# Second batch's keys and values in the places of eight weight tiles, and a softmax constant added by ScalarE

## The chip, the cores and the metric

One core of one Trainium2 chip runs the whole program. The metric is device time in microseconds (us) of one execution, as the median of several runs. A profile is one further execution, recorded instruction by instruction; its span runs from the first to the last instruction.

## The reference

```python
# B, H, S, D = 8, 8, 576, 64; pool = 8; Sp = 72
k_p = k.reshape(B, H, Sp, pool, D).mean(axis=3)
v_p = v.reshape(B, H, Sp, pool, D).mean(axis=3)
scores = scale * np.matmul(q, k_p.transpose(0, 1, 3, 2))
attn = np.exp(scores - np.max(scores, axis=-1, keepdims=True))
attn = attn / (np.sum(attn, axis=-1, keepdims=True) + 1e-09)
x = np.matmul(attn, v_p)              # -> (4608 tokens, 512)
h = np.maximum(np.maximum(x @ w1, x @ w2), x @ w3)    # 768 wide
x = h @ w_out                                         # 512 wide
h = np.maximum(x @ w_in, 0.0)                         # 2048 wide
out = h * h @ w_out2
```

The expert weights arrive as 64-bit numbers, which the kernel converts itself.

## The kernel before

**Three stages in one stream.** The 4608 tokens are cut into 12 blocks of 384. For block j, `attention(j)` (line 293) makes four x tiles, one per pair of heads; `moe1(j)` (line 529) multiplies them by w1, w2 and w3 (18 weight tiles, `w1_f_e` in the pool `w_p`, 6 chunks f by 3 matrices e), takes the maximum, and multiplies by the output weights `wo1` (6 tiles). Later stages (line 612 on) run the second expert layer with 512-token blocks and start when the first stage is done; the change doesn't touch them. A matmul product is split in three: high by high, high by low and low by high (`PARTS`), since every operand is held as a high half, rounded by ScalarE (line 135), and a low half, which is the rest (line 136, by VectorE, for weights by GpSimd).

**Weights.** A weight tile is loaded raw (line 147, 512 KB, 64-bit integers) on SP's queue, into one of four places `raw0` to `raw3`. `convert` (line 150) turns it into floats with two ScalarE operations (lines 162 and 163) and two VectorE operations (lines 164 and 167), and `split` makes the two halves. While `shared[0]` is true, that is until the last output weight has been loaded, the four raw places go round in turn for weights, keys and values together (`place`, line 127).

**Attention.** A block holds pieces of one batch or two: block 0 is the first 384 tokens of batch 0, block 1 the last 192 of batch 0 and the first 192 of batch 1, block 2 the rest of batch 1. Batch 0's values are pooled by matmuls (line 264). From batch 1 on, `load_k` (229) and `load_v` (234) load one pair's keys (288 KB) and values (288 KB), `prepare_k` (239) sums groups of eight on VectorE (line 241) and scales them into `kbd` on ScalarE (244), and `prepare_v` (246) does the like for values (lines 248, 215 and 216). `softmax` (359) computes scores on TensorE (367), the maximum on VectorE (369), and exponentials with their sums on ScalarE (372, one activation and one read of its accumulator per tile and head). Then come the added constant (376) and the reciprocal (377) on VectorE, and the product of both on GpSimd (378). `transpose` (lines 399 and 408) and `values` (426 for batch 0, 437 and 438 later) make the x tile. The 64 softmaxes have 64 of the added constants. Ahead of the second layer's weights, the program also converts those and stores them (from line 451 on), in the course of blocks 2 to 11.

**What sets the order.** All steps go into the list `todo` with a due time in matmul steps of a block (`STEPS` is 22, of which 18 are weight tiles and four output columns) and are emitted in that order; loads lead their softmax by `LEAD_LOAD` = 10 steps. The framework's scheduler then orders the instructions of each engine from its own model of their costs, so a changed cost or a changed dependence moves instructions far from the edit. Each engine, SP's queue too, runs its own list strictly in order. A tile of a pool with a tag takes the place of the tile that had the tag before, and its writer waits until that one's readers are done.

Of the kernel before, what the change touches and what calls it, by code (L numbers as in the profile page):

```python
# [10 lines left out]
F32 = mybir.dt.float32  # L11
# [3 lines left out]
AF = mybir.ActivationFunctionType  # L15
# [5 lines left out]
P = 128  # L21
B, H, S, D = 8, 8, 576, 64
POOL = 8
SP = S // POOL
NPAIR = H // 2
# [4 lines left out]
KF1 = FF1 // P  # L30
FF2 = 2048
KF2 = FF2 // P
NE = 3
# [52 lines left out]
def as_f32(ap):  # L86
    return ap.bitcast(F32)
# [8 lines left out]
def attention_moe_kernel(ctx: ExitStack, tc: tile.TileContext, q, k, v, vn, w1, w2, w3, wo1, wi2, wo2, out):  # L96
    nc = tc.nc
# [29 lines left out]
    def place(kind):  # L127
        if shared[0]:
            turns["both"] += 1
            return f"raw{turns['both'] % 4}"  # L130
        turns[kind] += 1
        return f"raw{2 * kind + turns[kind] % 2}"
# [48 lines left out]
    w_p = s1.enter_context(tc.tile_pool(name="w_p", bufs=1))  # L181
# [6 lines left out]
    raw_p = s_at.enter_context(tc.tile_pool(name="raw_p", bufs=4, side="right"))  # L188
# [35 lines left out]
    def early(shape, name):  # L224
        if unused:
            return w_p.tile(shape, F32, tag=unused.pop(0), name=name)
        return raw_p.tile(shape, F32, tag=place(1), name=name, bufs=1)

    def load_k(b, p):
        kr = raw_p.tile([P, 2 * 512], F32, tag=place(1), name="kr", bufs=1)[:, :S]  # L230
        nc.sync.dma_start(out=kr, in_=k[b, p])
        return kr

    def load_v(b, p):
        vr = raw_p.tile([P, 2, D, POOL], F32, tag=place(1), name="vr", bufs=1)[:SP]
        nc.sync.dma_start(out=vr, in_=v[b - NATURAL, :, 2 * p : 2 * p + 2])
        return vr

# [7 lines left out]
    def prepare_v(p, vr):  # L246
        vs = sm_p.tile([SP, 2, D], F32, tag="vs", name="vs", bufs=2)
        nc.vector.tensor_reduce(out=vs, in_=vr, axis=AX.X, op=ALU.add)
        split_scaled(vst[:, p, 0:4:3], vst[:, p, 1:3], vs, V_SCALE)
# [75 lines left out]
    def scores(g):  # L325

        if not used or used[-1][1] + g > 3:
            used.append([sm_p.tile([P, 3, 2, SP], F32, tag="ss", name="ss", bufs=3), 0])
        used[-1][1] += g
        return used[-1][0][:, used[-1][1] - g : used[-1][1]]  # L330

    def attend(j, b, s0, n, p, t):

        kr, vr, qr, pt, sms = [], [], [], [], []
# [3 lines left out]
        def load():  # L338
            if j == 0:
                kq = early([P, 2 * 512], "kq")  # L340
                kr.append(kq[:, :S])
                qr.append(kq[:, S : S + n])
                nc.sync.dma_start(out=kr[0], in_=k[b, p])
            elif first:
                kr.append(load_k(b, p))
            if j:
                qr.append(raw_p.tile([P, T1], F32, tag="qr", name="qr", bufs=4)[:, :n])
            nc.sync.dma_start(out=qr[0], in_=q[b, p, :, s0 : s0 + n])
            if first and b >= NATURAL:
                vr.append(load_v(b, p))  # L350
# [8 lines left out]
        def softmax():  # L359
            if vr:  # L360
                prepare_v(p, vr.pop())
            g = len(tiles)
            sc = sc_ps.tile([P, 3 * 2 * SP], F32, tag="sc", name="sc")
            ss = scores(g)[:m]
            src = sc[:, : g * 2 * SP].rearrange("p (g h s) -> p g h s", h=2, s=SP)[:m]
            for i, (c, _) in enumerate(tiles):
                nc.tensor.matmul(src[:, i], lhsT=qr[0][:, c : c + m], rhs=kbd[:, p], start=True, stop=True)  # L367
            st = sm_p.tile([P, 3, 3, 2], F32, tag="st", name="st")[:m, :, :g]
            nc.vector.tensor_reduce(out=st[:, 0], in_=src, axis=AX.X, op=ALU.max, negate=True)  # L369
            for i in range(g):  # L370
                for h in range(2):
                    nc.scalar.activation(  # L372
                        ss[:, i, h], src[:, i, h], AF.Exp, bias=st[:, 0, i, h : h + 1],
                        accum_out=st[:, 1, i, h : h + 1],
                    )
            nc.vector.tensor_scalar_add(st[:, 1], st[:, 1], 1e-9)
            nc.vector.reciprocal(st[:, 2], st[:, 1])  # L377
            nc.gpsimd.tensor_tensor(  # L378
                out=ss, in0=ss,
                in1=st[:, 2].rearrange("p g (h o) -> p g h o", o=1).to_broadcast([m, g, 2, SP]), op=ALU.mult,  # L380
            )
            sms.append(ss)
# [36 lines left out]
        def values():  # L419
# [22 lines left out]
            split(x, xf)  # L442

        return load, prepare, softmax, carry, transpose, values

    w1_t, wo1_t = {}, {}
# [454 lines left out]
```

## Time and profile before

| | us |
|---|---|
| median of 3 runs (1459.45 to 1472.45) | 1459.91 |
| the profiled execution | 1462.14 |
| its span, first to last instruction | 1459.7 |
| TensorE matmuls busy in the span | 1425.5 |
| VectorE | 977.9 |
| ScalarE | 759.4 |
| GpSimd | 182.9 |

In the profile PE is the matmul side of TensorE and PEld its weight loads, DVE is VectorE, ACT is ScalarE, POOL is GpSimd and SPq the queue of DMA issues on SyncE. A matmul in plain fp32 counts as two instructions in the trace. Matmuls overlap, so the busy time of one is longer than its share; the count of instructions per microsecond tells more. PEclk is the TensorE clock that was granted, as a share of 2.4 GHz. The weights of the first layer are converted in the first 115 us, while blocks 0 and 1 are computed.

### The profile page before, as it was taken

To read this page: it belongs to the slowest core of one execution; us is meant where nothing else is said; L and a number is where in the kernel's file an instruction comes from. 1 tells how busy PE (TensorE), PEld (TensorE's weight loads), DVE (VectorE), ACT (ScalarE), POOL (GpSimd) and SP (SyncE) were. 2 spreads that over 40 slices of the span, in tenths; PEclk is the share of its full clock that TensorE was granted. 3 is DMA by queue.
4 is the path that set the end of the run, shared out by engine and by line. 5 is a ranking of instruction groups with operands and counts; after the bars stand their busy time and mean duration, and the time that the engine had idled before them with its cause. 6 is when DMAs were issued, how large, how long until landed. Compare 5 with 4: busy or idle time off the path is not lost.

```text
span 1459.7 us, 27670 instructions
## 1 busy us (share of the span) xinstructions
PE 1425.5 (98%) x10410; PEld 1403.0 (96%) x10410; DVE 977.9 (67%) x1754; ACT 759.4 (52%) x1959; POOL 182.9 (13%) x229
## 2 busy tenths in 40 slices
PE   6889999999999999999999999999999999999998
PEld 4879999999999999999999999999999999999998
DVE  5887477656675756646336767686867767686865
ACT  7795366655665657655223544453535444454543
POOL 3441022212322222221000000000000000000000
PEclk9989999999999999999999999999999999999999
DMA  7554145444455444433459747566566666555746
GB/s 226 182 169 141 62 143 180 162 140 142 146 180 177 149 148 142 133 120 107 167 190 355 290 160 256 186 223 222 209 221 224 232 231 221 204 217 199 258 153 209
DMA packets 125029, 272.81 MB, mean 187 GB/s; under 512 B 13504, under 2 KB 69568, under 8 KB 124896
## 3 DMA queue, kind: packets, MB, share of 16 engines
q1 hardware_dynamic: 117984, 261.61, 52.8%
q10 hardware_dynamic: 6912, 9.44, 1.8%
q8 instruction: 82, 1.34, 0.4%
q14 instruction: 51, 0.42, 0.1%
HBM read 213.91 MB, written 48.23 MB: 180 GB/s over the span
## 4 chain that ended last, share of the span: by engine, by line
PE 77%; DMA 5%; DVE 2%; ACT 1%; issue 1%; SPq 0%; POOL 0%; ACTq 0%; DVEq 0%; POOLq 0%
PE ps L701 23%; PE ps L541 22%; PE ps L560 8%; PE accB L825 6%; PE accA L825 6%; PE accE L825 3%; PE accF L825 3%; DMA wo2s<-wo_dram 3%; PE accD L825 2%; PE sc L367 2%; PE av L438 1%; PE av L437 1%; DMA wraw<-in_wi_dram 0%; PE tr L408 0%; DMA yr<-y_dram 0%
## 5 line engine op out<-in xcount | busy, mean ns | idle before, releaser
L541 PE MATMUL ps<-x,w 128*128 128x384 f32 x2592 | 491.0, 342 | 5.5 <-ACT w L135 3.0
L541 PEld LDWEIGHTS ps<-x,w 128*128 128x128 f32 x2592 | 452.0, 190 | 8.3 <-ACT w L135 3.4
L701 PE MATMUL ps<-y,wi2s 128*128 128x256 f32 x3024 | 372.8, 278 | 0.7 <-DVE a L672 0.2
L701 PEld LDWEIGHTS ps<-y,wi2s 128*128 128x128 f32 x3024 | 357.2, 188 | 2.4 <-DVE c L672 1.3
L560 PE MATMUL ps<-h,wo 128*128 128x384 f32 x864 | 159.0, 337 | 0.1
L560 PEld LDWEIGHTS ps<-h,wo 128*128 128x128 f32 x864 | 149.6, 188 | 0.3 <-ACT wo L135 0.2
L714 ACT ACTIVATE c<-c 128x512 f32<-128x512 f32 x90 | 56.3, 626 | 168.6 <-DVE c L672 168.0
L672 DVE TENSOR_TENSOR c<-ps,c 128x512 f32<-128x512 f32 x144 | 98.2, 687 | 66.4 <-PE ps L701 63.5
L549 DVE TENSOR_TENSOR hm<-ps,hm 128x384 f32<-128x384 f32 x144 | 79.7, 553 | 81.3 <-PE ps L541 78.8
L135 ACT ACTIVATE g<-c 128x512 fp32r<-128x512 f32 x144 | 90.3, 627 | 57.0 <-DVE c L711 23.3
L825 PE MATMUL accA<-wo2s,g 128*128 128x256 f32 x864 | 115.6, 277 | 0.0
L825 PE MATMUL accB<-wo2s,g 128*128 128x256 f32 x864 | 111.7, 279 | 3.9 <-DMA wo2s<-wo_dram 3.0
L372 ACT ACTIVATE ss<-sc,st 128x72 f32<-128x72 f32 (+1 forms) x320 | 97.8, 320 | 29.9 <-DVE st L369 24.8
L825 PEld LDWEIGHTS accB<-wo2s,g 128*128 128x128 f32 x864 | 104.5, 189 | 4.9 <-ACT g L135 2.2
L136 DVE TENSOR_TENSOR g<-c,g 128x512 fp32r<-128x512 f32 x144 | 97.8, 686 | 16.4 <-ACT g L135 16.4
L825 PEld LDWEIGHTS accA<-wo2s,g 128*128 128x128 f32 x864 | 107.0, 188 | 0.0
L441 DVE TENSOR_TENSOR xf<-av,xf 64x192 f32<-64x192 f32 (+1 forms) x112 | 50.7, 452 | 39.3 <-ACT xf L440 37.6
L378 POOL TENSOR_TENSOR ss<-ss,st 128x432 f32<-128x432 f32 (+1 forms) x64 | 53.1, 830 | 178.3 <-DVE st L377 95.0
L135 ACT ACTIVATE h<-hm 128x384 fp32r<-128x384 f32 x72 | 37.6, 522 | 56.2 <-DVE hm L549 55.5
L372 ACT ACTIVATION_READ_ACCUMULATOR ss<-sc,st 128x1 f32 (+1 forms) x320 | 66.2, 207 | 0.0
L135 ACT ACTIVATE g<-s 128x512 fp32r<-128x512 f32 x72 | 44.3, 630 | 35.3 <-DVE s L675 17.5
L163 ACT ACTIVATE wraw<-wraw 128x512 int32<-128x512 uint32 x56 | 37.8, 675 | 43.4 <-DMA wraw<-in_wi_dram 16.4
(111 smaller groups left out, 1929.2 us busy)
## 6 DMA issues: line engine op xcount, KB each, us to landing
wo2s<-wo_dram SPq DMA_DIRECT2D x252, 512.0 KB, 5.8
wi2s<-wi_dram SPq DMA_DIRECT2D x24, 512.0 KB, 6.5
wraw<-in_wo_dram SPq DMA_DIRECT2D x22, 512.0 KB, 3.9
wraw<-in_w_dram SPq DMA_DIRECT2D x18, 512.0 KB, 5.2
y_dram<-ys ACTq DMA_DIRECT2D x48, 192.0 KB, 2.7
wraw<-in_wi_dram SPq DMA_DIRECT2D x16, 512.0 KB, 3.7
wi_dram<-wraw SPq DMA_DIRECT2D x16, 512.0 KB, 3.0
wo_dram<-wraw SPq DMA_DIRECT2D x64, 128.0 KB, 2.1
```

The lines of the kernel that those rows point to most:

```text
L135: nc.scalar.activation(hi, src, AF.Copy)
L136: engine.tensor_tensor(out=lo, in0=src, in1=as_f32(hi), op=ALU.subtract)
L372: nc.scalar.activation(ss[:, i, h], src[:, i, h], AF.Exp, bias=st[:, 0, i, h : h + 1], accum_out=st[:, 1, i, h : h + 1],)
L378: nc.gpsimd.tensor_tensor(out=ss, in0=ss, in1=st[:, 2].rearrange("p g (h o) -> p g h o", o=1).to_broadcast([m, g, 2, SP]), op=ALU.mult,)
L441: nc.vector.tensor_tensor(out=xf[r], in0=av[r], in1=xf[r], op=ALU.add)
L541: nc.tensor.matmul(ps, lhsT=w1_t[f, e][:, a, kk * P : (kk + 1) * P], rhs=x[kk][:, c], start=(n == 0), stop=(n == 3 * KD - 1),)
L549: nc.vector.tensor_tensor(out=hm, in0=ps, in1=hm, op=ALU.max)
L560: nc.tensor.matmul(ps, lhsT=wo1_t[kk][:, a, d * P : (d + 1) * P], rhs=hs[kk][:, c], start=(n == 0), stop=(n == 3 * KF1 - 1),)
L672: nc.vector.tensor_tensor(out=out, in0=in0, in1=in1, op=ALU.add)
L701: nc.tensor.matmul(bank[:, u * HT : (u + 1) * HT], lhsT=wi2_t[2 * gr + u][i][:, a, o + kk * P : o + (kk + 1) * P], rhs=y_t[j][m][:, c, kk] ...
L714: nc.scalar.activation(c, c, AF.Relu)
L825: nc.tensor.matmul(bank[:, i * 256 : (i + 1) * 256], lhsT=g[:, a, u * HT + i * P : u * HT + (i + 1) * P], rhs=w[:, u, c], start=(n == 0 an ...
```

## The change

There are two edits. Batch 1's keys and values (4 pairs, 8 tiles) no longer take raw places: pair p's keys take the place of weight tile number 10 + 2p of the 18 and its values that of number 11 + 2p, which are `w1_3_1` to `w1_5_2`, before these weights are written. So that such a load isn't issued at the very start, `behind_weights` has GpSimd copy one element of the low half of weight tile number 2p (keys) or 2p + 1 (values) into the place first; the load waits for that copy. Later batches use the raw places as before. The second edit is in `softmax`: the constant 1e-9 is added by a ScalarE activation (Copy with a bias) instead of a VectorE addition.

```diff
+    def kv_place(b, i):
+
+        if b > 1:
+            return raw_p, place(1)
+        f, e = divmod(NE * KF1 - 2 * NPAIR + i, NE)
+        return w_p, f"w1_{f}_{e}"
+
+    def behind_weights(b, i, dst):
+        if b == 1:
+            nc.gpsimd.tensor_copy(dst, as_f32(w1_t[divmod(i, NE)][:1, 1, :1]))
+
     def load_k(b, p):
-        kr = raw_p.tile([P, 2 * 512], F32, tag=place(1), name="kr", bufs=1)[:, :S]
+        pool, tag = kv_place(b, 2 * p)
+        kr = pool.tile([P, 2 * 512], F32, tag=tag, name="kr", bufs=1)[:, :S]
+        behind_weights(b, 2 * p, kr[:1, :1])
         nc.sync.dma_start(out=kr, in_=k[b, p])
         return kr
 
     def load_v(b, p):
-        vr = raw_p.tile([P, 2, D, POOL], F32, tag=place(1), name="vr", bufs=1)[:SP]
+        pool, tag = kv_place(b, 2 * p + 1)
+        vr = pool.tile([P, 2, D, POOL], F32, tag=tag, name="vr", bufs=1)[:SP]
+        behind_weights(b, 2 * p + 1, vr[:1, 0, 0, :1])
         nc.sync.dma_start(out=vr, in_=v[b - NATURAL, :, 2 * p : 2 * p + 2])
         return vr
...
-            nc.vector.tensor_scalar_add(st[:, 1], st[:, 1], 1e-9)
+            nc.scalar.activation(st[:, 1], st[:, 1], AF.Copy, bias=1e-9)
             nc.vector.reciprocal(st[:, 2], st[:, 1])
```

From `load_k` on the lines of the changed kernel stand 10 to 15 higher than those of before; lines that the text names are those of before. The engines' orders change in many places up to the end of the first stage, and three of them follow. A name like `w_2_0_477` is weight tile f = 2, e = 0 with its buffer's number; `kr` is a load of keys, `vr` of values, `wraw` of raw weights, `qr` of queries.

SP's queue, from the first raw weights on, before:

```order
L147 DMA wraw<-in_w_dram 128x1024 x2
L348 DMA qr<-in_q_dram 128x192
L147 DMA wraw<-in_w_dram 128x1024 x2
L231 DMA kr<-in_k_dram 128x576
L348 DMA qr<-in_q_dram 128x192
L231 DMA kr<-in_k_dram 128x576
L236 DMA vr<-in_v_dram 72x1024
L147 DMA wraw<-in_w_dram 128x1024
L231 DMA kr<-in_k_dram 128x576
```

The same place now:

```order
L147 DMA wraw<-in_w_dram 128x1024 x2
L363 DMA qr<-in_q_dram 128x192
L147 DMA wraw<-in_w_dram 128x1024 x2
L363 DMA qr<-in_q_dram 128x192
L147 DMA wraw<-in_w_dram 128x1024 x3
L244 DMA kr<-in_k_dram 128x576
L363 DMA qr<-in_q_dram 128x192
L251 DMA vr<-in_v_dram 72x1024
L363 DMA qr<-in_q_dram 128x192
L244 DMA kr<-in_k_dram 128x576
L147 DMA wraw<-in_w_dram 128x1024
```

Seven raw weights stand ahead of the first keys instead of four.

TensorE, around the scores of batch 1's fourth pair (the last row of scores with 96 tokens), before:

```order
L541 MATMUL ps<-x,w_1_0_413 128x384 x12
L408 MATMUL tr<-ident,ss 72x96 x2
L541 MATMUL ps<-x,w_1_1_429 128x384 x10
L367 MATMUL sc<-kbd,qr 96x144 x2
L541 MATMUL ps<-x,w_1_1_429 128x384 x2
L541 MATMUL ps<-x,w_1_2_452 128x384
```

The same place now:

```order
L556 MATMUL ps<-x,w_1_0_413 128x384 x12
L441 MATMUL av_612<-pt,vst_f 128x192 x2
L556 MATMUL ps<-x,w_1_1_431 128x384 x12
L556 MATMUL ps<-x,w_1_2_454 128x384 x12
L423 MATMUL tr<-ident,ss 72x96 x2
L556 MATMUL ps<-x,w_2_0_481 128x384 x5
L382 MATMUL sc<-kbd,qr 96x144 x2
```

Those scores stand behind five matmuls of w_2_0 instead of inside w_1_1.

TensorE, around the last av matmuls of block 1 (`av` with 128x192; L541 are expert products, L560 the output product), before:

```order
L541 MATMUL ps<-x,w_5_2_848 128x384 x2
L437 MATMUL av_1052<-pt,vst 128x192
L438 MATMUL av_1052<-pt,vst 128x192
L560 MATMUL ps<-h,wo_0_900 128x384 x2
L541 MATMUL ps<-x,w_0_0_362 128x384 x6
L541 MATMUL ps<-x,w_5_2_848 128x384 x10
L437 MATMUL av_1057<-pt,vst 128x192
L438 MATMUL av_1057<-pt,vst 128x192
```

The same place now:

```order
L575 MATMUL ps<-h,wo_4_1031 128x384
L556 MATMUL ps<-x,w_0_0_362 128x384 x2
L556 MATMUL ps<-x,w_0_1_378 128x384 x2
L452 MATMUL av_1000<-pt,vst 128x192
L453 MATMUL av_1000<-pt,vst 128x192
L382 MATMUL sc<-kbd,qr 128x144 x3
L575 MATMUL ps<-h,wo_5_1072 128x384 x2
L452 MATMUL av_1060<-pt,vst 128x192
L453 MATMUL av_1060<-pt,vst 128x192
L452 MATMUL av_1065<-pt,vst 128x192
L453 MATMUL av_1065<-pt,vst 128x192
```

Block 0's expert products and most of its first output column now stand ahead of the last av.

## Rows read from the trace of the kernel before

**Rows 1.** Windows: from:to length, busy us (instructions) by engine, PEclk, DMA share, GB/s
```profile
0.00:28.50 28.50, 17.96 (x68) 10.88 (x69) 14.33 (x28) 18.88 (x82) 8.06 (x17) 0.91 0.73 233
28.50:53.00 24.50, 18.64 (x94) 14.92 (x93) 19.30 (x43) 18.92 (x68) 11.55 (x11) 0.90 0.69 213
53.00:75.00 22.00, 21.83 (x136) 21.28 (x136) 19.09 (x38) 17.92 (x64) 9.63 (x9) 1.00 0.51 158
75.00:100.50 25.50, 20.89 (x105) 18.61 (x105) 23.20 (x45) 23.70 (x78) 12.69 (x10) 0.87 0.58 189
100.50:112.30 11.80, 10.60 (x53) 10.17 (x54) 9.39 (x16) 9.60 (x20) 6.02 (x6) 0.86 0.34 103
112.30:140.00 27.70, 27.70 (x170) 27.48 (x169) 18.32 (x35) 14.94 (x54) 5.72 (x5) 1.00 0.51 156
```

**Rows 2.** Waits of TensorE from 125 us to the end: total us, times, longest
```profile
PE ps L541 <- DVE hm L549: 0.8, 1, 0.8
```

**Rows 3.** Timeline, last x of block 1: start us, us, engine line op [idle before]
```profile
105.41 0.28 PE L438 MATMUL av<-pt,vst 72*128 72x192 f32 x1
...
107.96 0.36 ACT L135 ACTIVATE x<-xf 128x192 fp32r<-128x192 f32 x1 [0.17 <-DVE xf L441]
...
110.71 0.35 DVE L136 TENSOR_TENSOR x<-xf,x 128x192 fp32r<-128x192 f32 x1
...
111.11 0.96 PE L541 MATMUL ps<-x,w 128*128 128x384 f32 x4 [1.18 <-DVE x L136]
```

**Rows 4.** ScalarE by line and shape, 10 to 115 us: count | busy us, mean ns
```profile
L372 ACT ACTIVATION_READ_ACCUMULATOR ss<-sc,st 96x1 f32 x32 | 6.8, 212 | 0.0
...
L244 ACT ACTIVATE kbd<-ks 64x72 f32<-64x72 f32 x14 | 3.7, 264 | 2.6 <-DVE ks L241 2.5
...
L135 ACT ACTIVATE wo<-wbits 128x512 fp32r<-128x512 f32 x5 | 3.1, 625 | 0.4 <-DVE wbits L167 0.4
```

**Rows 5.** Timeline of ScalarE, a relu and the square that reads its result
```profile
853.16 0.63 ACT L714 ACTIVATE c<-c 128x512 f32<-128x512 f32 x1 [8.58 <-DVE c L672]
853.82 0.63 ACT L715 ACTIVATE c<-c 128x512 f32<-128x512 f32 x1
```

**Rows 6.** VectorE by line and shape, 10 to 115 us
```profile
L167 DVE SCALAR_TENSOR_TENSOR wbits<-wraw,wbits 128x512 int32<-128x512 int32 x23 | 17.6, 763 | 0.1
...
L248 DVE TENSOR_REDUCE vs<-vr 72x128 f32<-72x1024 f32 x5 | 6.1, 1213 | 3.2 <-DMA vr<-in_v_dram 3.2
...
L241 DVE TENSOR_REDUCE ks<-kr 128x72 f32<-128x576 f32 x5 | 3.7, 743 | 2.3 <-DMA kr<-in_k_dram 2.3
...
L376 DVE TENSOR_SCALAR st<-st 128x6 f32<-128x6 f32 x8 | 3.1, 393 | 1.7 <-ACT ss L372 1.7
...
L376 DVE TENSOR_SCALAR st<-st 96x4 f32<-96x4 f32 x8 | 2.9, 356 | 0.0
```

**Rows 7.** Timeline, a slow addition on VectorE and GpSimd beside it
```profile
26.20 2.15 POOL L136 TENSOR_TENSOR w<-wbits,w 128x512 fp32r<-128x512 f32 x1 [2.33 <-ACT w L135]
...
27.11 1.26 DVE L376 TENSOR_SCALAR st<-st 128x6 f32<-128x6 f32 x1
```

**Rows 8.** Timeline of SP's queue, first keys and fifth raw weights
```profile
21.07 0.33 SPq L231 DMA_DIRECT2D kr<-in_k_dram  x1
...
27.26 0.36 SPq L147 DMA_DIRECT2D wraw<-in_w_dram  x1
```

**Rows 9.** Waits of ScalarE for raw weights, 10 to 115 us
```profile
ACT wbits L162 <- DMA wraw<-in_w_dram: 4.5, 4, 1.8
...
ACT wraw L163 <- DMA wraw<-in_wo_dram: 1.8, 2, 1.4
```

**Rows 10.** w_2_0's low half, the landing of keys (KB, median us), and the fourth pair's scores
```profile
kr<-in_k_dram SPq DMA_DIRECT2D x8, 288.0 KB, 3.1
...
56.33 1.30 POOL L136 TENSOR_TENSOR w<-wbits,w 128x512 fp32r<-128x512 f32 x1
...
57.18 0.65 PE L367 MATMUL sc<-kbd,qr 128*96 128x144 f32 x4
```

## Prediction

> **What bounds the kernel now.** I read first where TensorE loses time, in windows over the span, then who it waits for, then the two engines that feed it there. From 112 us on it is never short: the window to 140 us has 27.70 us busy out of 27.70, and after 125 us the first expert product waits for a feeder engine only once, 0.8 us for the running maximum [rows 1, 2]. The loss lies ahead of that. In the two full windows (53 to 75 and 112.3 to 140 us) an instruction of TensorE comes every 22.0/136 = 0.162 and 27.7/170 = 0.163 us; I take 0.163 as its price, an estimate for the mixture there. At that price the 94 instructions of 28.5 to 53 us needed 15.3 us of 24.5, the 105 of 75 to 100.5 us 17.1 of 25.5, the 53 of 100.5 to 112.3 us 8.6 of 11.8 [rows 1]. That is 9.2 + 8.4 + 3.2 = 20.8 us lost between the first expert matmul and saturation. The granted clock (0.90, 0.87, 0.86 of full speed in those three, 1.00 in the full ones) is a part of that sum. The first 28.5 us hold other shapes and are not priced; the change reorders little there. So what can be won is some 20 us, 1.4% of the span, and most of it hangs on VectorE and ScalarE: in 75 to 100.5 us they are busy 23.20 and 23.70 us of 25.5 [rows 1].
>
> TensorE becomes saturated when block 1's last x is there. In the trace its last av matmul stands at 105.41 us, ScalarE writes that x's high half at 107.96, VectorE its low half only at 110.71, and the matmul that waited starts at 111.11 [rows 3]. I ask how this moment moves, and how much matmul work is already behind TensorE by then.
>
> **The change part by part.** *What the order does on TensorE.* Ahead of the last av of block 1 stand, before, 222 expert matmuls (L541) and 2 of the output product (L560); now 228 and 17, and three more score matmuls, which the trace counts as six instructions. These 21 + 6 = 27 at 0.163 us are 4.4 us of work done before the same event instead of after it: **-4.4**.
>
> *What stands ahead of the last x on ScalarE.* Before, 222 instructions; now 250, counted in the order: three more high halves of output weights, one more bit conversion, one output copy, six more scaled keys, and 16 of the new additions. Three weights, the conversion and the copy I price alike at 0.63 (the copy is no larger), less the 0.1 by which neighbours overlap: 5 x 0.53 = 2.6. Six keys at 0.26 are 1.6 [rows 4]. The addition is not in the trace. It waits for its own engine's accumulator, as the square at L715 waits for the relu at L714: these start 0.66 apart with 0.63 busy, so such a wait costs the overlap and 0.03 [rows 5]. The bounds for the addition are 0.1 (the accumulator read's 0.21 less overlap) and 0.4 (the smallest key, 0.26, with its wait); I take 0.2, nearest the accumulator read, which is as small a tile [rows 4]. 16 x 0.2 = 3.2. Sum **+7.4** (5.8 to 10.6).
>
> *What leaves VectorE.* 16 additions of that stretch took 3.1 + 2.9 = 6.0 us, 0.375 each, for tiles of six or four elements a partition: one at 27.11 us took 1.26 and ended at 28.37, with GpSimd's 26.20 + 2.15 = 28.35 beside it [rows 6, 7]. Those stalls go with the instruction. Against it, VectorE has ahead of the last x two more L167 and one more L164 (3 x 0.76), three more key sums (3 x 0.74), two more value sums (2 x 1.21) and two maxima, priced as key sums: 2.3 + 2.2 + 2.4 + 1.5 = 8.4 [rows 6]. Its queue grows by 8.4 - 6.0 = 2.4, ScalarE's by 7.4. VectorE was 2.75 us behind ScalarE at the last x [rows 3]; with 5.0 less growth it no longer is, and what remains late is ScalarE's half. I credit the gap less the 0.35 which VectorE needs itself: **-2.4** (0 to -6.0).
>
> *The loads.* Keys and values of batch 1 no longer take raw places. SP's fifth weight load was issued at 27.26 us, behind a key load that had taken a place at 21.07; now three weight loads stand ahead of the first key [rows 8]. ScalarE waited 4.5 us for raw weights of the first product and 1.8 for those of the output weights [rows 9]. I take the first as gone and keep the second, because batch 2's keys still share the places then: **-4.5** (0 to -6.3).
>
> *The added wait.* Each of the eight loads now waits for a one-element copy on GpSimd that reads one of the first eight weights' low halves. SP is in order, so weight loads 8 to 14 stand behind those waits too, but a raw load waits anyway until a later weight has been converted; I cost that at nothing, and at one landing time of 3.1 us if that cover is gone [rows 10]. The wait that can show is the fourth key: it needs the low half of w_2_0, which before ended at 56.33 + 1.30 = 57.6. Then 0.4 for copy and issue, 3.1 landing, 0.74 for the sum, 0.53 for both scaled keys: 62.4 [rows 4, 6, 10]. TensorE asked for those scores at 57.18 [rows 10]; now 77 expert matmuls stand ahead of them instead of 58, 19 x 0.163 = 3.1, so at 60.3. **+2.1** (0 if the weights come two microseconds earlier, 5.1 if they come three later). The eight places themselves are asked for by their weights tens of matmuls after the keys are summed; no wait there.
>
> *Later.* The other 48 additions cross to ScalarE while TensorE never waits for it [rows 2]: nothing, within 0.8 us. What hides them is TensorE's own full queue; without it they would cost 48 x 0.2 = 9.6.
>
> Sum: -4.4 + 7.4 - 2.4 - 4.5 + 2.1 = **-1.8 us**. The profiled execution took 1462.14 us (span 1459.7 and 2.4 around it), 2.2 above the median of 1459.91; against its own time that is 1460.3, and against the median, which I predict, **1458.1**.
>
> A rule speaks against the second edit. The Trainium skill, page "ScalarE: Activation LUTs", section "Rules for kernel authors", sends additions to VectorE and not to ScalarE. Its section "What ACT_TABLE_LOAD costs" gives 186 ns and 0.833 ns per element for an activation with immediate constants, of which 93 ns overlap; by that the addition is an estimated 0.1 us and the sum 1.6 lower. By the rule alone, with nothing returned by VectorE, the sum would be +0.6. The trace sides with the edit for this stretch: 0.375 us each on VectorE against bounds of 0.1 to 0.4.
>
> **The rivals.** *All the waits go.* Weight loads early, the addition at 0.1, no port stalls, no wait for the fourth key: -4.4 + 5.8 - 6.0 - 6.3 = -10.9, 1449.0. For it: the order has most weights earlier against keys and values. Against: ScalarE and VectorE are nearly full, and an engine that is full does not gain from earlier data.
>
> *The keys come too late (slower).* The keys now hang on weights which hang on the same two full engines. If raw loads bring ScalarE nothing, w_2_0's low half ends three microseconds later than it did; TensorE, in order, stands at the fourth pair's scores for 5.1 us with all of w_2_0's rest behind them, and the chain of block 1's x moves with it: -4.4 + 7.4 - 2.4 + 5.1 = +5.7, 1465.6. It decides from the point where that half ends after 55.5 us (60.3 less the 4.8 from copy to keys). For it: block 0's fourth x has more ScalarE work ahead than before. Against: the order has w_2_0 about where it was on ScalarE.
>
> *The places don't limit.* SP's waits at raw loads end mostly with VectorE's conversion, so a free place may come no earlier in effect, and the reordering cancels: 1459.9.
>
> **How the numbers follow.** Forecast 0.48, all waits gone 0.2, keys too late 0.22, no effect 0.1. A measurement here tells about 1% from no change, 14.6 us. The best bound is -10.9 and the worst is -4.4 + 10.6 + 5.1 = +11.3, both inside 1%. Beyond it I leave a twentieth on each side: for a second stall of the same kind, since 20.8 us are at stake in all, or for an order that hides more than I count. The range takes in the second case nearly whole and the third: 1450 to 1466; the forecast's own is 1454 to 1461.
>
> **What would show it.** Right: the fifth weight load issued some 5 us earlier, ScalarE's wait for raw weights in 10 to 115 us below 2 us; the last x of block 1 between 107 and 115 us with 15 or more output matmuls ahead of it; the additions on ScalarE near 0.2 us; everything after 115 us as before. Wrong: a gap of several microseconds on TensorE at the last batch-1 scores, in front of w_2_0's matmuls; or gaps in front of the output product because its weights are late; or a difference that arises after 140 us.

## The result: 8 us slower where 2 us faster were forecast

| | runs | median, us | lowest to highest |
|---|---|---|---|
| before | 19 | 1460.61 | 1456.93 to 1472.45 |
| changed | 19 | 1469.62 | 1465.12 to 1473.38 |

The ratio is 1.0056, with a 95% interval of 1.0045 to 1.0066: 8.2 us (6.6 to 9.6) slower by the ratio, 9.0 by the two medians. The profiled execution took 1472.27 us, its span is 1470.6.

### The profile page after: what moved, and what is told of

It reads as the page before. It is cut to its first block, busy times and chain, and to the rows that moved or that the text cites. A ratio compares the mean times of both kernels' runs of the same rounds, so it can differ in the third digit from the quotient of the medians.

```text
span 1470.6 us, 27639 instructions
## 1 busy us (share of the span) xinstructions
PE 1429.2 (97%) x10410; PEld 1403.0 (95%) x10410; DVE 972.0 (66%) x1690; ACT 767.8 (52%) x2023; POOL 190.7 (13%) x237
## 4 chain that ended last, share of the span: by engine, by line
PE 80%; DMA 7%; DVE 5%; ACT 4%; issue 3%; POOL 1%; SPq 0%; ACTq 0%; POOLq 0%; DVEq 0%
PE ps L556 25%; PE ps L716 22%; PE ps L575 8%; PE accA L840 6%; PE accB L840 6%; DMA wo2s<-wo_dram 4%; PE accE L840 3%; PE accF L840 3%; PE accD L840 2%; PE sc L382 2%; ACT ss L387 1%; DMA wraw<-in_wo_dram 1%; PE av L452 1%; PE av L453 1%; DVE wbits L164 1%
## 5 line engine op out<-in xcount | busy, mean ns | idle before, releaser
L135 ACT ACTIVATE g<-c 128x512 fp32r<-128x512 f32 x144 | 90.2, 627 | 57.1 <-DVE c L726 23.3
L393 POOL TENSOR_TENSOR ss<-ss,st 128x432 f32<-128x432 f32 (+1 forms) x64 | 63.3, 989 | 201.7 <-DVE st L392 178.2
L455 ACT ACTIVATE xf<-av 64x192 f32<-64x192 f32 (+1 forms) x112 | 45.5, 406 | 40.1 <-PE av L453 31.8
L135 ACT ACTIVATE h<-hm 128x384 fp32r<-128x384 f32 x72 | 37.5, 521 | 53.2 <-DVE hm L564 52.7
L135 ACT ACTIVATE g<-s 128x512 fp32r<-128x512 f32 x72 | 44.4, 630 | 35.2 <-DVE s L690 17.5
```

The costliest lines, as they stand in the source:

```text
L135: nc.scalar.activation(hi, src, AF.Copy)
L393: nc.gpsimd.tensor_tensor(out=ss, in0=ss, in1=st[:, 2].rearrange("p g (h o) -> p g h o", o=1).to_broadcast([m, g, 2, SP]), op=ALU.mult,)
```

## The profile after

The windows of [rows 1] for the changed kernel, in the same columns, and the length from 140 to 200 us behind them:

```profile
0.00:28.50 28.50, 16.86 (x59) 9.48 (x60) 11.95 (x21) 18.99 (x84) 7.22 (x17) 0.94 0.75 240
28.50:53.00 24.50, 20.67 (x93) 16.13 (x91) 17.25 (x35) 20.43 (x78) 15.55 (x17) 0.79 0.66 205
53.00:75.00 22.00, 18.72 (x110) 17.69 (x111) 19.97 (x33) 16.70 (x51) 10.45 (x10) 1.00 0.56 168
75.00:100.50 25.50, 22.83 (x133) 20.57 (x132) 24.57 (x40) 23.22 (x73) 14.70 (x11) 1.00 0.62 196
100.50:112.30 11.80, 8.21 (x37) 6.57 (x38) 9.59 (x16) 7.36 (x26) 5.18 (x4) 0.77 0.39 118
112.30:140.00 27.70, 26.62 (x140) 25.86 (x140) 13.25 (x28) 12.33 (x47) 4.10 (x4) 0.85 0.34 101
140.00:200.00 60.00, 60.00 (x367) 59.45 (x367) 31.79 (x59) 27.35 (x77) 3.74 (x6) 1.00 0.24 79
```

Read the counts behind PE. From 53 to 75 us TensorE starts 110 instructions instead of 136, and from 100.5 to 140 us 37 + 140 instead of 53 + 170; from 75 to 100.5 us it starts 133 instead of 105. The first 140 us hold 567 instructions, against 622 in one window over the same stretch before. At the forecast's price of 0.163 us the missing 55 are 9.0 us, most of the 10.9 by which the spans differ. From 140 us on TensorE is full again. Note where the 55 are: 36 are missing by 75 us (59 + 93 + 110 against 68 + 94 + 136), but 28 of these are made up by 100.5 us, and 46 more go missing from there to 140 us. Most of the loss that stays is made behind 100.5 us, on the way to block 1's last x and just behind it.

The event that the forecast is built on, block 1's last x, as in [rows 3] (start, us, engine, line; lines stand 15 higher now):

```profile
118.81 0.41 PE L453 MATMUL av<-pt,vst 72*128 72x192 f32 x1
...
122.73 0.36 ACT L135 ACTIVATE x<-xf 128x192 fp32r<-128x192 f32 x1
123.12 0.36 DVE L136 TENSOR_TENSOR x<-xf,x 128x192 fp32r<-128x192 f32 x1 [0.43 <-ACT x L135]
```

Its last av matmul stands at 118.81 us instead of 105.41, and ScalarE writes the high half at 122.73 instead of 107.96. Two windows of the changed kernel ahead of it and around it, and the first of them before (third row):

```profile
104.00:116.00 12.00, 7.58 (x26) 5.96 (x27) 11.79 (x21) 6.50 (x25) 5.12 (x5) 0.62 0.38 115
112.30:125.00 12.70, 11.62 (x52) 10.91 (x52) 7.94 (x19) 6.21 (x24) 3.19 (x3) 0.68 0.35 102
...
104.00:116.00 12.00, 10.82 (x65) 10.23 (x63) 11.66 (x20) 7.83 (x17) 5.12 (x4) 0.96 0.31 93
```

From 104 to 116 us TensorE starts 26 instructions, 4.2 us of work at the forecast's price, and VectorE is full: busy 11.79 us of 12.00. Before, VectorE was as full in those 12 us (11.66), and TensorE started 65. So it isn't how much VectorE has to do there, but what it does first. From 112.3 to 125 us TensorE has 52 instructions; before it had 84. It shows 11.62 us busy with so few: the granted clock is 0.68 of 2.4 GHz there, while before it was 1.00.

What stands ahead on VectorE shows in its value sums of batch 2, the first two in the changed kernel and the first one before (third row):

```profile
103.67 1.22 DVE L263 TENSOR_REDUCE vs<-vr 72x128 f32<-72x1024 f32 x1 [2.00 <-DMA vr<-in_v_dram]
...
108.30 1.22 DVE L263 TENSOR_REDUCE vs<-vr 72x128 f32<-72x1024 f32 x1
...
111.58 1.21 DVE L248 TENSOR_REDUCE vs<-vr 72x128 f32<-72x1024 f32 x1
```

Before, that sum came behind the last x, whose low half was made at 110.71 us [rows 3]. Now two of them stand ahead of it, and VectorE, which runs its list in order, waits 2.00 us idle for the first one's values to land, with block 1's x behind them.

Whom TensorE waits for, from 75 to 140 us (total us, times, longest):

```profile
PE ps L556 <- DVE hm L564: 3.1, 3, 2.1
PE ps L556 <- DVE x L136: 1.1, 1, 1.1
PE av L452 <- DVE pt L428: 1.0, 1, 1.0
PE tr L423 <- DVE xf L456: 0.8, 1, 0.8
```

No single wait answers for it, but the smaller ones that follow (0.5 and 0.5 us for VectorE, 0.2 for ScalarE) make 7.2 us in all, and 7.0 of these are for VectorE. Before, in the same stretch, the largest were 3.0 us for weights (ScalarE's half, L135) and 1.2 for an x.

The parts that the forecast priced. The addition on ScalarE (L391 now), VectorE's second bit operation and GpSimd's softmax product, each from 10 to 115 us by line and shape:

```profile
L391 ACT ACTIVATE st<-st 128x6 f32<-128x6 f32 x8 | 1.8, 220 | 0.0
L391 ACT ACTIVATE st<-st 96x4 f32<-96x4 f32 x8 | 1.7, 206 | 0.0
```

```profile
L167 DVE SCALAR_TENSOR_TENSOR wbits<-wraw,wbits 128x512 int32<-128x512 int32 x24 | 21.5, 897 | 0.1
```

```profile
L393 POOL TENSOR_TENSOR ss<-ss,st 96x288 f32<-96x288 f32 x8 | 8.5, 1066 | 9.5 <-DVE st L392 9.5
...
L393 POOL TENSOR_TENSOR ss<-ss,st 128x432 f32<-128x432 f32 x7 | 7.4, 1054 | 23.9 <-DVE st L392 21.4 <-issue 2.5
```

The product before, in the same stretch:

```profile
L378 POOL TENSOR_TENSOR ss<-ss,st 128x432 f32<-128x432 f32 x8 | 7.9, 987 | 27.2 <-DVE st L377 26.4 <-POOL w L136 0.8
...
L378 POOL TENSOR_TENSOR ss<-ss,st 96x288 f32<-96x288 f32 x8 | 6.2, 778 | 9.3 <-ACT w L135 3.7 <-DVE st L377 3.6 <-DVE st L376 1.1
```

The addition costs 0.220 and 0.206 us. But L167, which the change doesn't touch, takes 897 ns instead of 763 [rows 6], and the product, which took 778 ns in its smaller shape and 987 in the larger, takes 1066 and 1054.

The raw weights: ScalarE's waits as in [rows 9], then the issues as in [rows 8], then what SP's queue waits for ahead of them, all from 10 to 115 us:

```profile
ACT wraw L163 <- DMA wraw<-in_w_dram: 4.5, 4, 1.7
...
ACT wraw L163 <- DMA wraw<-in_wo_dram: 0.7, 1, 0.7
```

```profile
23.07 3.78 SPq L147 DMA_DIRECT2D wraw<-in_w_dram  x3
28.72 0.33 SPq L244 DMA_DIRECT2D kr<-in_k_dram  x1
```

```profile
SPq L147 <- DVE wbits L167: 41.9, 17, 4.9
```

Weights five to seven are issued from 23.07 to 26.85 us, the fifth 4 us earlier than before, and yet ScalarE waits 4.5 + 0.7 us for raw weights, where it had waited 4.5 + 1.8. The last row points to the reason: SP waits 41.9 us for places that VectorE's L167 has still to read. Before, that was 37.1 us in 16 waits, with 4.9 us more behind a landing of values, which is gone now. Most of these waits weren't for keys and values before either.

The fourth pair's scores, as in [rows 10], with the instructions ahead of them:

```profile
63.59 0.33 PE L423 MATMUL tr<-ident,ss 96*72 96x96 f32 x2
63.70 1.12 PE L556 MATMUL ps<-x,w 128*128 128x384 f32 x5
64.66 0.65 PE L382 MATMUL sc<-kbd,qr 128*96 128x144 f32 x4
```

They start at 64.66 us, and no row shows a wait in front of them.

## The experiments

Theories on record: A, the addition costs time on ScalarE; B, the keys come too late behind their gates; C, the scheduler makes another order for every changed program, and the order decides; later D, the places themselves cost. Each ratio is against runs of the kernel before on the same chip.

### Each edit alone

The places alone (the diff shown ahead, without the `softmax` line), the places without the gates, the addition alone, and the whole change without the gates. The gate's edit is:

```diff
-        behind_weights(b, 2 * p, kr[:1, :1])
...
-        behind_weights(b, 2 * p + 1, vr[:1, 0, 0, :1])
```

Places alone: 

> Batch 1's keys and values in the weights' places with their gates; the constant stays on VectorE. Theory A (the constant on ScalarE costs the time: ScalarE is full in the first 115 us and VectorE's stalls only move to its neighbours): within 2 us of before. Theory B (keys gated by weights reach TensorE late): 5 to 9 us slower than before, ratio 1.003 to 1.006. Theory C (each edit reshuffles the scheduler's order, and the order decides): a value that neither edit explains, the two single edits not adding up to the whole change.

Places without gates: 

> Keys and values in the weights' places but without the copies that gate them, the constant on VectorE: the loads are issued as SP's order has them. Theory A: within 2 us of before and of the places with gates. Theory B: at least 5 us faster than the places with gates, at or below before. Theory C: any value, with the last x of block 1 moving as the time does.

Addition alone: 

> The constant on ScalarE alone; keys and values in the raw places as before. Theory A: 5 to 9 us slower than before, ratio 1.003 to 1.006. Theory B: within 2 us of before. Theory C: as for the places alone, the two differences don't add up to 8 us.

All without gates: 

> The changed kernel without the gating copies. Theory A: as slow as the changed kernel, ratio to before 1.004 to 1.007. Theory B: 5 us or more faster than the changed kernel, near before. Theory C: any value.

| kernel | median, us | ratio, 95% | TensorE instructions in 140 us | last av of block 1, us |
|---|---|---|---|---|
| places alone | 1465.59 | 1.0035 (1.002 to 1.005) | 591 | 112.40 |
| places, no gates | 1466.69 | 1.0044 (1.0026 to 1.0062) | 600 | 108.88 |
| addition alone | 1468.05 | 1.0056 (1.0036 to 1.0076) | 586 | 111.82 |
| all, no gates | 1467.53 | 1.0048 (1.003 to 1.0066) | 604 | 112.43 |

Theory B falls: without gates nothing clear of the noise is regained. Each edit alone loses 5 to 8 us, and both together lose no more than the addition. Losses of instructions would add up; these don't.

### No addition at all

The constant is left out, so the reciprocal reads the sums as they are.

```diff
-            nc.vector.tensor_scalar_add(st[:, 1], st[:, 1], 1e-9)
             nc.vector.reciprocal(st[:, 2], st[:, 1])
```

> The constant is not added at all (the softmax sums go to the reciprocal as they are): 64 instructions less than the kernel before, none of them on ScalarE, and the scheduler free to order anew. Theory A: as the kernel before or up to 6 us faster (0.996 to 1.000), since VectorE is relieved and ScalarE carries nothing more. Theory C: the time follows the new order, whatever the work: anything from 0.996 to 1.007, and slower than the kernel before would be understood by theory C alone.

Measured: 1467.90 us, 1.0032 (1.0015 to 1.0048), 588 instructions in 140 us. A program with 64 instructions less and none more is 4.7 us slower. Of the theories on record only C allows that.

### The order held

To separate an instruction's cost from the order, a table of instruction numbers, taken from the built program whose order is wanted (`ORDER`, a row for each engine, SP's queue too), is added as dependences without semaphores, so that the scheduler has no choice left:

```diff
+def hold_order(tc):
...
+    for row in ORDER:
+        for a, b in zip(row, row[1:]):
+            tc.add_manual_dep(table[f"I-{b}"], f"I-{a}", info, reason="order")
```

Addition on ScalarE, order of before: 

> The kernel before with the order of its instructions held as it was on every engine; only the 64 additions of the small constant go from VectorE to ScalarE, each right behind its group's last exponential. Theory A (the addition costs time on ScalarE, and VectorE's relief gives nothing back): slower by about 7 us, 1.0045 to 1.006, like the addition alone with a free scheduler. Theory C (the time is set by the order that the scheduler makes of the changed program, not by what the instruction costs): within 2 us of the kernel before, 0.9985 to 1.0015, the last weighted sum of block 1 on TensorE at 104 to 107 us.

Addition on VectorE, order of the addition alone: 

> The addition stays on VectorE, but all engines keep the order that the scheduler made for the kernel with the addition on ScalarE. Theory A: as the kernel before, 0.9985 to 1.0015. Theory C: as the addition alone, 1.004 to 1.007 (6 to 10 us slower), the last weighted sum of block 1 at 110 us or later.

Changed kernel's order, addition back: 

> The changed kernel with its order held on all engines, places and gates as changed, only the 64 additions back on VectorE, each ahead of its reciprocal. Theory A: 3 to 5 us less than the changed kernel, 1.0025 to 1.0035 of the kernel before, as the places alone. Theory C: as the changed kernel, 1.0045 to 1.0066.

| addition on | in the order of | median, us | ratio, 95% | instructions in 140 us |
|---|---|---|---|---|
| ScalarE | before | 1462.26 | 0.9989 (0.9974 to 1.0003) | 620 |
| VectorE | addition alone | 1477.06 | 1.0086 (1.0061 to 1.011) | 567 |
| VectorE | changed kernel | 1477.97 | 1.0096 (1.0069 to 1.0123) | 559 |

One row of the windows for the first and one for the second of them, in the columns of [rows 1]:

```profile
0.00:140.00 140.00, 120.19 (x620) 104.75 (x621) 96.37 (x182) 107.01 (x378) 53.26 (x55) 0.91 0.60 184
```

```profile
0.00:140.00 140.00, 111.19 (x567) 95.59 (x568) 100.92 (x185) 96.88 (x335) 51.29 (x54) 0.90 0.57 177
```

The traces show the orders as they were meant: against the run whose order is held, and the addition aside, TensorE, VectorE, GpSimd and SP's queue run the same instructions in the same sequence, and ScalarE but for 14 places from 120 us on in the first kernel. A kernel held in its own order with nothing else changed wasn't run.

The first is the kernel before with the new addition, and loses nothing. The second is the kernel before, instruction for instruction, in another order, and is 12.6 us slower, with 55 instructions less in 140 us. Both slow kernels are slower than theory C expected of them (1.007 and 1.0066 at most), the third clear of the noise, so the order isn't all. Theory A falls: in the other two orders the addition measured better on ScalarE, 1.0056 against 1.0086 in the addition alone's, where the two intervals overlap, and 1.0056 against 1.0096 in the changed kernel's, where they don't.

### Both edits in the order of before

The places can't be held in that order as they stand: without the keys' turns the weights rotate into other raw places. So the keys and values of batch 1 still count as turns, and the gates are left out. The changed kernel itself, with its own rotation, wasn't tried in the order of before.

```diff
+        if b == 1:
+            place(1)
         f, e = divmod(NE * KF1 - 2 * NPAIR + i, NE)
```

Both edits: 

> Both edits, without the gating copies, with every engine held to the order of the kernel before, and the second batch's keys and values still counting as turns in the rotation of the raw places, so that each weight comes into the place it had before. Theory C (the order decides): within 3 us of the kernel before, 0.998 to 1.002, the last weighted sum of block 1 at 104 to 107 us. Theory D (the places themselves cost, whatever the order): 4 to 7 us slower, 1.003 to 1.005. If only the raw weights' waits count: 2 to 4 us faster, 0.997 to 0.9985, ScalarE's waits for wraw below 3 us in the first 140 us, against 6.3 in the profile of the kernel before.

Places alone: 

> The places alone, without the gating copies, the addition on VectorE, with every engine held to the order of the kernel before, the rotation of the raw places as before. Theory C: within 3 us of the kernel before, 0.998 to 1.002. Theory D: 4 to 7 us slower, 1.003 to 1.005, like the places with a free scheduler (1.0035 and 1.0044).

Measured: both 1460.79 us, **0.9976 (0.996 to 0.9991)**, 640 instructions in 140 us, last av of block 1 at 101.00; places alone 1461.56, 0.9989 (0.9975 to 1.0002), 635 and 103.15. Both edits in the old order are 3.5 us faster than before, the one kernel of the study that is faster clear of the noise. That is a little more than theory C expected (0.998), and the last av came 3 us ahead of the 104 to 107 that it expected. Theory D falls. ScalarE's waits for raw weights, 10 to 115 us, in it:

```profile
ACT wbits L179 <- DMA wraw<-in_w_dram: 3.8, 4, 1.3
...
ACT wraw L180 <- DMA wraw<-in_wo_dram: 0.8, 1, 0.8
```

They are 4.6 us against 6.3 [rows 9], where below 3 had been expected if the raw weights alone counted. The addition alone in the old order, whose raw places are those of before, has 3.6, so the fall isn't shown to be the places' work.

### Where in the order

For the addition alone, the order of before up to a given instruction of TensorE, the other order behind it, and once the reverse; the code is as above, only the table differs.

Before's to 75 us: 

> The addition on ScalarE; all engines in the order of the kernel before up to TensorE's 298th instruction (75 us there), from then on in the order that the scheduler made for the addition alone. If the cost lies in what that order does after 75 us (work that fills the waits spent too early, the last weighted sums later): 1.003 to 1.007. If it lies ahead of it: 0.999 to 1.002.

Reverse: 

> The reverse: the order of the addition alone up to TensorE's 276th instruction (75 us there), from then on the order of the kernel before. If the cost lies after 75 us: 0.998 to 1.002, the last weighted sum of block 1 back near 105 us. If it lies ahead of it: 1.003 to 1.007.

To 90 us: 

> As the cut at 75 us, but the order of the kernel before is kept up to TensorE's 358th instruction (90 us there), past the transposes and the first two weighted sums of block 1. If the late attention of block 1 costs: 0.999 to 1.003, most of the loss gone. If what stands behind costs: 1.005 to 1.009.

To 100 us: 

> As the cuts at 75 and 90 us (1.0088 and 1.0089), but the order of the kernel before is kept up to TensorE's 401st instruction (100 us there). If the loss comes from the order ahead of 100 us: 0.999 to 1.003. If it comes from what follows: 1.006 to 1.010.

To 112 us: 

> The same with the cut at TensorE's 455th instruction (112 us there), behind the last weighted sum of block 1. The orders go on differing behind it, on TensorE up to its 4972nd instruction. If the loss is made before 112 us: 0.999 to 1.003, TensorE full from 112 us on as in the kernel before. If the order behind 112 us costs as well: 1.004 or more.

| order | median, us | ratio, 95% | last av of block 1, us |
|---|---|---|---|
| before's, from 75 us the other | 1476.97 | 1.0088 (1.0068 to 1.0108) | 115.46 |
| the other, from 75 us before's | 1466.12 | 1.0021 (1.0007 to 1.0035) | 105.15 |
| before's, from 90 us the other | 1474.45 | 1.0089 (1.0069 to 1.0109) | 111.94 |
| before's, from 100 us the other | 1476.14 | 1.0091 (1.007 to 1.0112) | 101.91 |
| before's, from 112 us the other | 1469.08 | 1.0041 (1.0022 to 1.006) | 103.72 |

TensorE's longest waits from 75 to 150 us, in turn with the cut at 75, 90, 100 and 112 us:

```profile
PE tr L425 <- DVE xf L458: 3.8, 2, 3.6
PE av L454 <- DVE xf L458: 3.2, 3, 2.0
```

```profile
PE ps L577 <- ACT wo L152: 6.2, 2, 4.7
```

```profile
PE sc L384 <- ACT kbd L261: 6.1, 2, 5.5
```

```profile
PE ps L558 <- ACT ys L583: 3.2, 1, 3.2
```

Most of that order's loss is in what it does behind 75 us, since the old order from there on brings the 1.0056 of the addition alone down to 1.0021. But the first row, 1.0088, measured more than that order as a whole (the intervals overlap) and more than was expected of the cut (1.007), so joining two orders may cost too. Wherever the two are joined, another wait appears: 7.0 us for VectorE's copies of x, 6.2 for an output weight, 6.1 for scaled keys, 3.2 for an output copy. With the cut at 100 us block 1's last av is as early as 101.91, and the kernel as slow as any: an early event doesn't bring the time.

Three tables then moved one kind of work alone, as far as both orders allow:

Attention forward in the slow order: 

> The addition on ScalarE. Up to 75 us the order of the kernel before, from there the order that the scheduler made for the addition alone (which measured 1.0088 with that cut), but with all instructions of the attention moved forward on their engines to where the kernel before had them, as far as both orders allow: the transposes of block 1 (L425 here) stand at TensorE's 305th instruction again instead of the 341st, its first weighted sum at the 343rd instead of the 367th. If the late attention of block 1 is what costs: 1.000 to 1.004, at least half of the loss gone. If it is something else of that order: 1.006 to 1.010.

Attention back in the old order: 

> The reverse: the order of the kernel before, with the addition on ScalarE, but from 75 us on all instructions of the attention moved back on their engines towards where the other order has them: the transposes of block 1 at TensorE's 330th instruction instead of the 305th, its first weighted sum at the 358th instead of the 334th, hidden-layer matmuls ahead of them. If the late attention costs: 1.004 to 1.009. If it is something else: 0.998 to 1.002.

Weights forward in the old order: 

> The order of the kernel before, with the addition on ScalarE, but from 75 us on the preparation of the weights moved forward on ScalarE, VectorE and GpSimd towards where the other order has it (1 to 11 places); TensorE's first 700 instructions stand as before. If weights ahead of the attention on ScalarE and VectorE are enough to lose the time: 1.003 to 1.007. If only TensorE's order counts: 0.998 to 1.002.

Measured: 1474.04 us and 1.0088 (1.0068 to 1.0107); 1476.19 and 1.0102 (1.0084 to 1.012); 1465.67 and 1.0027 (1.0015 to 1.004). Attention moved back loses all of it, yet moved forward it wins none of it back; weights moved forward, with TensorE's first 700 instructions as they were, lose 3.9 us. The second is beyond the 1.009 that was expected, the third between its two expected ranges. So the loss isn't shown to be one kind of work in a wrong place.

One item recurs in the traces. In eight slow kernels VectorE runs batch 2's first value sum ahead of block 1's last x and waits 1.5 to 3.8 us for its values: the changed kernel (2.00), its order with the addition back (1.90), the addition alone (3.73), its order with the addition on VectorE (2.85), no addition (3.79), and the cuts at 75 (2.21) and 90 us (2.75); the attention moved forward has it still (1.54). In the kernels that keep the order of before there, the sum comes behind that x. But the places alone and the attention moved back are slow without such a wait, the whole change without gates with one of 0.43, and the cut at 100 us with the sum behind. No run moves these sums alone, so what they are worth isn't shown. Which of the moved instructions would be enough stays open, and the cuts were made in the order of the addition alone, not in the changed kernel's.

## Why the prediction was wrong

*The step that failed* is the one that had the event move by what is queued ahead of it. The order was read rightly: the 27 instructions that the first term (-4.4) has ahead of the event are there, and so are the counts on VectorE. The other terms, +7.4 - 2.4 - 4.5 + 2.1, let the last av move by +2.6 us; it moved by 118.81 - 105.41 = 13.4. Those 13.4 less the 4.4 of work done ahead of it are the 9.0 us that the counts show.

Two parts of that step went wrong, as the rows of all work up to the last x's low half show, before and in the changed kernel:

```profile
0.00:110.71 110.71, 88.74 (x447) 74.73 (x447) 83.72 (x163) 87.60 (x304) 47.18 (x50) 0.91 0.60 191
...
0.00:123.12 123.12, 97.03 (x468) 79.48 (x469) 90.81 (x157) 92.91 (x329) 56.28 (x61) 0.89 0.60 186
```

First, VectorE's queue was mis-sized: it grew by 90.81 - 83.72 = 7.1 us and not by 2.4. The 16 additions went as forecast, but the conversions ahead of the event (L164 and L167 together) came to 6.1 us more where 2.3 were counted, since each of them takes longer. Second, the waits: VectorE stands idle 32.3 us ahead of that x instead of 27.0, 5.3 more, where the forecast let the waits shrink. It priced the two more value sums at their work, 1.21 us each, and put the wait for their values at nothing; the first one's alone is 2.00 us. These 7.1 + 5.3 make the 12.4 us by which the low half is later. ScalarE's term was nearly right: busy 92.55 - 86.19 = 6.4 more up to its high half, against +7.4.

The worst bound, +11.3, holds the size, but the range stopped at 1466, short of it: the bounds of the queues were weighed, and the waits that a new order makes were not. And 0.56% can be told from no change here, where the forecast took 1% as needed.

*The edits themselves* go the way the forecast said. In the old order both give -3.5 us (-5.8 to -1.3). Their own terms, 16 x 0.2 = 3.2 for the additions, -2.4 and -4.5, make -3.7. That this comes so near is partly luck, for the parts fall otherwise: the addition alone gives -1.6 where 3.2 - 2.4 = +0.8 was counted, the places alone -1.6 where -4.5 was, and neither of the two is clear of zero. The order takes the rest, some 8.2 + 3.5 = 11.7 us. The forecast took the order for a list of extra instructions and not for a risk of its own.

Term by term:

- **Addition on ScalarE**, 0.2 within +7.4: right, 0.206 to 0.220. The rule of the Trainium skill that was weighed against the edit (page "ScalarE: Activation LUTs", section "Rules for kernel authors") sends additions to VectorE; in none of the three orders did the addition measure slower on ScalarE, and in two of them 4 to 6 us faster, in one clear of the noise. So the measurement goes against that rule for these small tiles.
- **VectorE relieved**, -2.4: the relief shows in the old order, and is absent in the new. With the additions gone and the order held, L164 and L167 (181 and 184 in that kernel) fall from 883 and 763 ns to 794 and 723, as its rows from 10 to 115 us show; with both edits in the old order they take 830 and 810, and in the new order L167 rises to 897. The sentence "Those stalls go with the instruction" holds only where the neighbours stay.

```profile
L181 DVE SCALAR_TENSOR_TENSOR wbits<-wbits,wraw 128x512 int32<-128x512 int32 x24 | 19.0, 794 | 7.1 <-ACT wraw L180 3.7 <-ACT wbits L179 2.7 <-issue 0.3
L184 DVE SCALAR_TENSOR_TENSOR wbits<-wraw,wbits 128x512 int32<-128x512 int32 x23 | 16.6, 723 | 0.1
```

- **Raw weights**, -4.5: mis-sized. The loads are issued as early as forecast, but the waits fell by 1.1 us, and by 1.7 in the old order. The third rival had the reason: SP's waits for raw places are mostly for VectorE's conversion, 41.9 us of them. Its time, 1459.9, was no nearer.
- **Fourth key behind its gate**, +2.1: nothing. In the changed kernel those scores run at 64.66 us without a wait in front of them. SP's queue does wait at the gates, 11.7 us for keys and 3.3 for values from 10 to 115 us, but without gates no time clear of the noise comes back. The rival of late keys had a near time, 1465.6, by a mechanism that didn't happen.
- **Later, nothing**: nearly so. TensorE is full from 140 us, but of the 10.9 us of span 1.9 arise there, and "within 0.8" was too narrow.

## What to carry to other kernels

Where a scheduler orders the program, first measure how much the order alone moves the time: the same instructions in the order of a slightly changed program. Here that was 12 us, while both edits together were worth 3.5. If an edit is worth less than that, hold the old order and test it there, or keep that order for good. Don't price a reordered stage by the sums of its queues alone: ask of each instruction that moves ahead whether its data will be there, and what stands behind it. And look for the full engine in short windows: VectorE seems to have room from 100.5 to 125 us (17.53 of 24.5), and is full for 12 us of them.

## What the runs showed of the hardware

The duration of an untouched VectorE operation follows the order: L167, one shape and 23 or 24 of them from 10 to 115 us, took 763 ns before, 723 with the additions gone and the order held, 810 with both edits in that order, 854 with the addition alone, 897 in the changed kernel and 987 without its gates. The difference lies in those that run beside GpSimd: the ones that overlap no GpSimd instruction took 672 to 692 ns before (13 of them) and 674 to 692 in the changed kernel (12), the ones that overlap one 870 on average before (10) and 1116 now (12). GpSimd's product grew with them. The Trainium skill, page "SBUF — State Buffer", section "Who interferes with whom", has a VectorE instruction with two inputs in SBUF contend with one of GpSimd that reads SBUF, and says "Issue order, not op shape, decides who blocks"; the trace agrees, with these numbers.

TensorE's clock fell in the starved stretch: in the changed kernel TensorE was busy 0.93 us of the 3 from 104 to 107 us, and from 107 to 120 us it was granted 0.50, the level of 1.2 GHz, with 39 instructions in 13 us. In 112.3 to 125 us it was granted 0.68 with 52 instructions, 1.00 with 84 before.
